# Dilated window attention followed by a multiplicative feed-forward: eight PSUM banks in one set, another turn of w3, another load order

## The chip, the cores and the metric

The kernel runs on one core of a Trainium2 chip. A core has five engines that work side by side, each with its own queue of instructions, done strictly in order: TensorE (PE) multiplies matrices; VectorE (DVE) and ScalarE (ACT) do elementwise work; GpSimd (POOL) here builds masks and issues the loads that convert fp32 to bf16 on the way; SyncE (SP) issues the stores and the DMA transposes. Engines wait for each other through semaphores. Operands lie in SBUF, and PE writes its results to PSUM, which has eight banks; a bank can be written again once its last reader is done. The metric is the device time of one execution in microseconds (us). The median before is 265.82 us (three runs, 264.5 to 266.85).

## The reference

```python
# q, k, v: (8 batches, 8 heads, 576 tokens, 64), fp32
scores = matmul(q, k^T) / 8
rel = pos[:, None] - pos[None, :]
mask_plain = (rel >= 0) & (rel < 32)                       # heads 0 to 3
mask_dil   = (rel >= 0) & (rel < 128) & (rel % 4 == 0)     # heads 4 to 7
attn = softmax(where(mask, scores, -1e9))
x = (attn @ v) as (4608 tokens, 512)
h = (x @ w1) * (x @ w2)              # w1, w2: 512 x 1024
out = (h @ w3) @ w_out               # w3: 1024 x 1024, w_out: 1024 x 512
```

A token sees 32 keys: the last 32 tokens (plain heads), or every fourth of the last 128 (dilated heads). Sorted by its remainder modulo 4, a dilated head is a plain one.

## The kernel before

**The tiling.** The 8 heads are two groups of four, `u` = 0 (plain) and `u` = 1 (dilated), and each group of a batch has six blocks of 96 queries against 128 keys. A `Step(b, u, hf)` is three blocks of four heads, so a batch has four steps, numbered 0 to 3 (0 and 1 are the plain halves, 2 and 3 the dilated ones). In the dilated group the tokens lie sorted by remainder, in runs of 144 (`RUN`), so step 2 holds the first two runs and step 3 the last two.

**One step.** q and k arrive as rows and are turned by DVE (`turn`, L289: whole, or in two parts for some shapes) to have the head dimension on the partitions. `scores` (L342) writes 24 small matmuls into a tile of four PSUM banks; for the first two batches (`BIASED`) four matmuls with an identity first add a mask as a bias. `exps` (L373) is one ACT exponential over 1152 columns; for the other batches `masks` (L377) multiplies the result by a 0/1 mask on DVE. `values` (L383) is 12 matmuls in two halves with a column of ones beside v, so that the sum of the weights comes along; `recip` and `norm` (L405, L419) divide, on DVE, in two halves. Then x is turned back: for the first two batches (`TURNED`) by PE and an ACT copy (`back`, `keep`, L441 and L450), for the others by a DMA transpose that SP issues (`back_dma`, L453). v comes for batches 0 and 1 as rows that DVE and PE turn (`v_back`, `v_keep`, L313 and L323), and for the others directly by strided loads (`load_v_plain`, `load_v_dil`), with a copy of the overlap (`halo_v`).

**The feed-forward.** The tokens are 16 units of 288, unit `k` being half `k % 2` of batch `k // 2`. Unit `k` needs steps 0, 1 and 2 + `k % 2` of its batch. For each unit and each of eight slices `f` of the hidden width, `up` (L470) makes four matmuls with w1, and four with w2; `copy_a` (ACT) and `gate` (DVE) multiply the two. `w3` and `w_out` are fused once: each of eight row slabs of w3 (256 KB in bf16) is turned (`w3_back` on PE, `w3_keep` on ACT) and multiplied by `w_out` (`w3_mul`, L539, then `w3_done`, L551). `down` (L496) multiplies a tile of 128 gated tokens with the fused weight; `copy_y` and `store` follow. Every `down` waits for all eight `w3_done`.

**The order.** It is written out by a planner (`Plan`, L50). Each piece of work is a task with an engine, an assumed duration, its dependences, an assumed latency to users on other engines and a priority; the planner walks through its own clock, gives each free engine the ready task of lowest priority number, and the instructions are then issued in that order. A task with `slot` also needs a free PSUM place. Before, there are four such places of one bank each (`ps_f`), and a separate tile of four banks for the scores (`ps_s`), so that a score step waits until the exponential before it has read the four banks. `RANK` sets the priorities of attention tasks, and `LEAD` how many batches attention runs ahead: the score step `i` of batch `b` comes after pair number `int(16 * (b - LEAD) + 4 * i)` of `up` (16 pairs a batch).

**The loads.** POOL issues, in this order: q, k, v of batch 0, group 0; identity and mask; q, k, v of group 1; w1 and w2, in two halves of 512 columns; w_out in two halves; the eight slabs of w3; q, k, v of batch 1; then the later batches as buffers come free. An issue waits until the load eight places earlier has landed.

Of the kernel before, what the change touches and what calls it, by code (L numbers as in the profile page):

```python
# [10 lines left out]
P = 128  # L11
# [8 lines left out]
S = 576  # L20
# [10 lines left out]
TURNED = 2  # L31
ORDER = (2, 3, 0, 1)
RANK = dict(E=2, VK=1.5, K=1.5, N=0.5, T=3, VT=0.1, S=0.3, V=0.3, X=0.3)
WARM = 16
VKE = (0, 0, 1, 1)
LEAD = 2.25
# [13 lines left out]
class Plan:  # L50
# [5 lines left out]
    def __init__(self, places):  # L56
        self.tasks, self.places, self.now = [], places, None

    def add(self, name, eng, dur, deps, fn, prio, slot=False, lat=150, after=()):
        t = Task(name, eng, dur, deps, fn, prio, slot, lat, after)  # L60
        self.tasks.append(t)
        return t

    def run(self):
# [15 lines left out]
        n, held = len(self.tasks), [None] * self.places  # L80
        now, order, dma = 0.0, [], 0.0

        def freed(t):
            ends = [u.end for u in takers[id(t)]] if t else []
            return None if None in ends else max(ends, default=-200.0) + 100

        while len(order) < n:
            progress = True
            while progress:
                progress = False  # L90
                for e in engines:
                    if free[e] > now:
                        continue
                    at = [freed(t) for t in held]
                    open_ = [(x, i) for i, x in enumerate(at) if x is not None and x <= now]
                    best = None
                    for r, t in waiting[e]:
                        if r > now or (t.slot and not open_):
                            continue
                        if best is None or t.prio < best[1].prio:  # L100
                            best = (r, t)
                    if best is None:
                        continue
                    t = best[1]
                    waiting[e].remove(best)
                    t.start = now
                    if e == "DMA":
                        free[e] = now + t.dur[0]
                        dma = max(dma, now + t.dur[0]) + t.dur[1]
                        t.end = dma + 1900  # L110
                    else:
                        t.end = free[e] = now + t.dur
                    if t.slot:
                        t.place = min(open_)[1]
                        held[t.place] = t
# [18 lines left out]
def kernel(  # L134
# [23 lines left out]
    plan = Plan(places=4)  # L158
# [4 lines left out]
    w3_pool = ctx.enter_context(tc.tile_pool(name="w3", bufs=8))  # L163
    ps_s = ctx.enter_context(tc.tile_pool(name="pss", bufs=1, space=bass.MemoryType.PSUM))
    ps_f = ctx.enter_context(tc.tile_pool(name="psf", bufs=1, space=bass.MemoryType.PSUM))
# [11 lines left out]
    mask = const.tile([P, 7, QB], BF16, name="mask")  # L177
    vps = [const.tile([P, H, 6, PITCH], BF16, name=f"vp{i}") for i in range(2)]
    bias = const.tile([P, 7, QB], BF16, name="bias")
    ets = [const.tile([P, 4 * VC + 32], BF16, name=f"et{i}") for i in range(4)]  # L180
# [5 lines left out]
    def bank(shape, dtype, name):  # L186
        return ps_f.tile(shape, dtype, tag=f"f{plan.now.place or 0}", name=name)
# [5 lines left out]
    def load_rows(nm, src, b, us):  # L193
        if (nm, b) not in qk:
            qk[(nm, b)] = qk_pool.tile([P, 2, 18 * D], BF16, tag=nm, name=nm)
        flat = src[b].rearrange("(u h) s d -> u (h s d)", u=2)
        flat = flat.rearrange("u (p x) -> p u x", p=P)
        nc.gpsimd.dma_start(out=qk[(nm, b)][:, us, :], in_=flat[:, us, :])

# [11 lines left out]
    def load_v_dil(b, m):  # L211
        vp = vps[b % 2]
        r, mu = 2 * (m // 3), m % 3
        runs = {
            0: [(0, 96, r, 0)],
            1: [(0, 48, r, 96), (48, 48, r + 1, 0)],
            2: [(0, 96, r + 1, 48)],
# [11 lines left out]
    def load_w(dst, src, c):  # L229
        f = slice(512 * c, 512 * (c + 1))  # L230
        nc.gpsimd.dma_start(
            out=dst[:, :, f], in_=src[:, f].rearrange("(a p) f -> p a f", p=P)
        )
# [32 lines left out]
    def blocks():  # L266
# [4 lines left out]
        by_res = base.rearrange("p (t r) -> p r t", r=4)  # L271
        nc.scalar.copy(
            out=bias[:, 0:4, :].rearrange("p i (r t) -> p i r t", r=4),
            in_=by_res.unsqueeze(1).to_broadcast([P, 4, 4, 24]),
        )
# [6 lines left out]
    def masks_of_bias():  # L282
        nc.vector.tensor_scalar(
            out=mask, in0=bias, scalar1=0.0, scalar2=None, op0=AL.is_ge
        )
# [3 lines left out]
    def turn(b, u, nm, part):  # L289

# [3 lines left out]
        if part is None:  # L294
# [3 lines left out]
        n, first, odd = ((5, 0, 2 * RUN + 4), (4, 2 * RUN, 5 - 2 * RUN))[part]  # L298
        o = bass.AP(
            tensor=d.tensor,  # L300
            offset=d.offset + pad + first,
            ap=[d.ap[0], [1, n], [RUN, 2], [9, 16], [odd, 2]],
# [3 lines left out]
            offset=src.offset + part * 64,  # L306
            ap=[src.ap[0], [128, n], [32, 2], [1, 32]],
# [5 lines left out]
    def v_back(b, u, half):  # L313
        x = bank([P, 3, 2, P], BF16, "vx")
# [8 lines left out]
    def v_keep(b, u, half, eng):  # L323
        dst = vps[b % 2][:, 4 * u : 4 * u + 4, 3 * half : 3 * half + 3, 0:D]
        for mm in range(3):
            o = dst[:, :, mm, :].rearrange("p h (j c) -> p h j c", c=2)
            i = spread[(b, u, half)][:, mm, :, :].rearrange("p c (h j) -> p h j c", h=4)
            if eng == "ACT":
                nc.scalar.copy(out=o, in_=i)
            else:  # L330
                nc.vector.tensor_copy(out=o, in_=i)  # L331

    class Step:
        def __init__(self, b, u, hf):
            self.b, self.u, self.hf = b, u, hf
            self.et = ets[2 * u + hf]

        def kind(self):
            first = 4 if self.u else self.hf
            return slice(first, first + 3)  # L340

        def scores(self, biased=False):  # L342
            b, u, hf = self.b, self.u, self.hf
            qt, kt = qts[b % 2], kts[b % 2]
            self.sp = ps_s.tile([P, 4, 512], F32, tag="s", name="sp")
            if biased:
                for g in range(4):
                    nc.tensor.matmul(  # L348
                        out=self.sp[:, g, 0:VC],
                        lhsT=ident,  # L350
                        rhs=bias[:, self.kind(), :],
# [3 lines left out]
            for mm in range(3):  # L355
                m = 3 * hf + mm
                for c in range(2):
                    for g in range(4):
# [4 lines left out]
                        else:  # L363
                            qq = qt[prt, u, QB * m : QB * m + QB, c]
                        nc.tensor.matmul(  # L365
                            out=self.sp[:, g, QB * mm : QB * mm + QB],
# [3 lines left out]
                            stop=(c == 1 and (mm == 2 or not biased)),  # L370
                        )

        def exps(self):  # L373
            ev = self.et[:, 0 : 4 * VC].rearrange("p (g x) -> p g x", g=4)
            nc.scalar.activation(out=ev, in_=self.sp[:, :, 0:VC], func=ACT.Exp, scale=scale)  # L375

        def masks(self):  # L377
            ev = self.et[:, 0 : 4 * VC].rearrange("p (g x) -> p g x", g=4)
            mk = mask[:, self.kind(), :].rearrange("p m x -> p (m x)")
            mk = mk.unsqueeze(1).to_broadcast([P, 4, VC])  # L380
            nc.vector.tensor_tensor(out=ev, in0=ev, in1=mk, op=AL.mult)  # L381

        def values(self, pg=None):  # L383

            vp = vps[self.b % 2]
            if pg is None:
                o = self.sp[:, :, VC : VC + 3 * (D + 1)].rearrange("p g (m e) -> p g m e", m=3)
                self.o = [o[:, 0:2, :, :], o[:, 2:4, :, :]]
                gs = range(4)
            else:  # L390
                if pg == 0:
                    self.o = [None, None]
                self.o[pg] = bank([P, 2, 3, D + 1], F32, "vo")
                gs = (2 * pg, 2 * pg + 1)
            for g in gs:
                for mm in range(3):
                    c0 = (3 * g + mm) * QB
                    nc.tensor.matmul(  # L398
                        out=self.o[g // 2][:, g % 2, mm, :],
                        lhsT=self.et[:, c0 : c0 + P],  # L400
                        rhs=vp[:, 4 * self.u + g, 3 * self.hf + mm, 0 : D + 1],
# [4 lines left out]
        def recip(self, pg=None):  # L406
            if pg in (None, 0):
                self.rcp = wk_pool.tile([P, 4, 3], F32, tag="rcp", bufs=4, name="rcp")
                self.xo = wk_pool.tile([P, 12 * D], BF16, tag="xo", bufs=4, name="xo")
            if pg is None:  # L410
                o = self.sp[0:QB, :, VC : VC + 3 * (D + 1)].rearrange(
                    "p g (m e) -> p g m e", m=3
                )
                nc.vector.reciprocal(out=self.rcp[0:QB, :, :], in_=o[:, :, :, D])
            else:
                nc.vector.reciprocal(  # L416
                    out=self.rcp[0:QB, 2 * pg : 2 * pg + 2, :], in_=self.o[pg][0:QB, :, :, D]
                )

        def norm(self, pg):  # L420
            gs = slice(2 * pg, 2 * pg + 2)
            if self.u == 0:
                dst = self.xo[0:QB, :].rearrange("p (m g d) -> p g m d", m=3, g=4)[:, gs, :, :]
            else:
                dst = self.xo[0:QB, :].rearrange("p (q m g d) -> p q g m d", q=2, m=3, g=2)
                dst = dst[:, pg, :, :, :]
            nc.vector.tensor_tensor(  # L427
                out=dst,
                in0=self.o[pg][0:QB, :, :, 0:D],
                in1=self.rcp[0:QB, gs, :].unsqueeze(3).to_broadcast([QB, 2, 3, D]),  # L430
# [10 lines left out]
        def back(self):  # L441
            self.x = bank([P, 6 * QB], BF16, "x")
# [7 lines left out]
        def keep(self):  # L450
            nc.scalar.copy(out=self.cols(), in_=self.x)  # L451
# [345 lines left out]
```

## Time and profile before

| | us |
|---|---|
| median of three runs | 265.82 |
| the profiled execution | 265.6 |
| its span | 263.8 |
| PE, DVE, ACT, POOL busy | 250.6, 172.6, 122.3, 62.7 |
| `up` matmuls (L473), first and last start | 23.1, 254.3 |
| `w3_back` on PE (L530), eight runs of 8 | 35.1 to 50.2 |
| DMA loads from 35 to 54 us | 205 GB/s |
| DMA from 200 to 254 us | 57 GB/s |

The profile is one execution. "PE" and "PEld" are the matmuls and the weight loads of TensorE. A group row gives the line, engine, operation, output from input with shapes and number, then busy time and the mean of one in ns, then idle time before it and what ended it. Matmuls overlap in their pipeline, so the pace of a run of matmuls is read from the chain of waits, which gives pieces as "start, length, what", and not from the mean of one. The busy rows of the page cut the span into 40 slices of 6.6 us, each a digit in tenths. The DMA rows give the time from issue to landing.

### The profile page before, as it was taken

The page shows a single profiled execution, that of the slowest core. Times are in us where ns is not written, and L with a number is a line of the kernel's source. Part 1 is how long each engine was busy: PE and PEld are TensorE (multiplying, and loading weights), DVE is VectorE, ACT ScalarE, POOL GpSimd, SP SyncE. Part 2 cuts the span into 40 slices and gives each one's busy share as a digit, 9 for nine tenths or more (in the row PEclk, how much of TensorE's full clock was granted, in tenths as well). Part 3 has the DMA queues.
Part 4 walks back from the last instruction along what each step waited for, and adds up shares of the span by engine and source line. Part 5 has one row for each costly group of instructions (what it writes and reads, how often), then busy time and mean ns, then how long its engine had stood idle before and what let it go on. Part 6 is the DMA issues. An engine that isn't in the chain of part 4 may idle for free.

```text
span 263.8 us, 6783 instructions
## 1 busy us (share of the span) xinstructions
PE 250.6 (95%) x2736; PEld 168.2 (64%) x2736; DVE 172.6 (65%) x383; ACT 122.3 (46%) x228; POOL 62.7 (24%) x98
## 2 busy tenths in 40 slices
PE   7477999999999999999999999999999999999993
PEld 3365775566667667657667676667676766777661
DVE  3986433899999899989898997455565322233320
ACT  3545354456738444653545444455452342433331
POOL 8612362241726436226313300000000000000000
PEclk9979999999999999999999999999999999999999
DMA  6999999999999959999999934225232112112113
GB/s 99 190 206 207 209 210 212 203 85 216 161 142 148 157 81 210 171 146 202 161 169 149 155 72 65 89 79 62 66 65 62 42 47 73 47 44 73 40 40 119
DMA packets 58030, 32.81 MB, mean 124 GB/s; under 512 B 44688, under 2 KB 47760, under 8 KB 58000
## 3 DMA queue, kind: packets, MB, share of 16 engines
q0 software_dynamic: 37776, 19.40, 58.1%
q1 hardware_dynamic: 20224, 12.98, 25.2%
q8 instruction: 21, 0.34, 0.5%
q14 instruction: 9, 0.07, 0.2%
HBM read 38.80 MB, written 9.44 MB: 183 GB/s over the span
## 4 chain that ended last, share of the span: by engine, by line
PE 77%; DMA 8%; DVE 7%; issue 3%; POOL 2%; ACT 1%; POOLq 0%; DVEq 0%; ACTq 0%
PE ab L473 43%; PE y L500 20%; DMA vp<-in_v_dram 5%; PE wf L542 5%; PE vo L398 3%; PE sp L365 3%; DMA qn<-in_q_dram 2%; DVE xo L427 1%; DVE qt L309 1%; PE x L530 1%; DVE vp L331 1%; DVE kt L309 1%; POOL vp L220 1%; PE sp L348 1%; PE x L444 1%
## 5 line engine op out<-in xcount | busy, mean ns | idle before, releaser
L473 PE MATMUL ab<-XT,w_sb 128*128 128x288 bf16 x1024 | 138.0, 286 | 1.2 <-ACT XT L451 0.7
L473 PEld LDWEIGHTS <-w_sb 128*128 128x128 bf16 x1024 | 96.5, 98 | 31.2 <-issue 1.7
L489 DVE TENSOR_TENSOR gt<-ab,asb 128x288 bf16<-128x288 f32 x128 | 57.9, 454 | 58.0 <-PE ab L473 56.2
L484 ACT CAST asb<-ab 128x288 bf16<-128x288 f32 x128 | 51.1, 400 | 50.6 <-PE ab L473 49.0
L500 PE MATMUL y<-wf_sb,gt 128*128 128x512 bf16 x288 | 67.7, 379 | 0.6 <-DVE vp L331 0.5
L511 ACT COPY osb<-y 128x512 f32<-128x512 f32 x36 | 21.1, 586 | 59.3 <-PE y L500 55.3
L500 PEld LDWEIGHTS <-gt 128*128 128x128 bf16 x288 | 27.8, 98 | 28.5 <-DVE vp L331 0.7
L375 ACT ACTIVATE et<-sp 128x1152 bf16<-128x1152 f32 x32 | 36.4, 1137 | 14.1 <-PE sp L365 14.1
L220 POOL DMA_DIRECT2D vp<-in_v_dram x48 | 31.4, 659 | 45.8 <-PE vo L398 17.7
L427 DVE TENSOR_TENSOR xo<-vo,rcp 96x384 bf16<-96x384 f32 x64 | 35.1, 551 | 1.9
L309 DVE STREAM_TRANSPOSE qt<-qn 128x320 uint32<-128x320 uint32 (+1 forms) x32 | 21.5, 681 | 3.3 <-DMA qn<-in_q_dram 3.0
L398 PEld LDWEIGHTS <-et 128*128 128x128 bf16 x384 | 15.9, 99 | 4.3 <-ACT et L375 0.9
L381 DVE TENSOR_TENSOR et<-et,mask 128x1152 bf16<-128x1152 bf16 x24 | 18.0, 752 | 1.0 <-ACT et L375 0.4
L398 PE MATMUL vo<-vp,et 128*128 128x65 bf16 x384 | 17.6, 195 | 0.9 <-ACT et L375 0.8
L416 DVE RECIPROCAL rcp<-vo 96x6 f32<-96x6 f32 x64 | 11.5, 182 | 8.3 <-PE vo L398 7.9
L542 PE MATMUL wf<-wo_sb,w3T 128*128 128x512 bf16 x64 | 15.0, 379 | 0.0
L365 PEld LDWEIGHTS <-kt 32*128 32x128 bf16 x768 | 9.6, 94 | 7.7 <-issue 7.2
L365 PE MATMUL sp<-qt,kt 32*128 32x96 bf16 x768 | 14.3, 204 | 0.0
L537 ACT COPY w3T<-x 128x1024 bf16<-128x1024 bf16 x8 | 8.1, 1012 | 7.7 <-PE x L530 7.6
L309 DVE STREAM_TRANSPOSE kt<-kn 128x320 uint32<-128x320 uint32 (+1 forms) x16 | 10.9, 681 | 0.1
L552 DVE CAST wf_sb<-wf 128x512 bf16<-128x512 f32 x8 | 5.5, 692 | 7.4 <-PE wf L542 7.4
L296 DVE STREAM_TRANSPOSE kt<-kn 128x576 uint32<-128x576 uint32 x8 | 9.9, 1240 | 0.0
(46 smaller groups left out, 104.2 us busy)
## 6 DMA issues: line engine op xcount, KB each, us to landing
qn<-in_q_dram POOLq DMA_DIRECT2D x7, 576.0 KB, 9.6
kn<-in_k_dram POOLq DMA_DIRECT2D x7, 576.0 KB, 7.9
w_sb<-in_moe_w_dram POOLq DMA_DIRECT2D x4, 512.0 KB, 13.6
w3n<-in_moe_w_dram POOLq DMA_DIRECT2D x8, 256.0 KB, 14.3
out_dram<-osb SPq DMA_DIRECT2D x8, 256.0 KB, 3.4
out_dram<-osb SPq DMA_DIRECT2D x8, 224.0 KB, 2.4
vp<-in_v_dram POOLq DMA_DIRECT2D x6, 288.0 KB, 12.9
out_dram<-osb SPq DMA_DIRECT2D x8, 192.0 KB, 2.5
```

Source lines behind the costliest of these rows:

```text
L220: nc.gpsimd.dma_start(out=vp[32 + p0 : 32 + p0 + n, 4:8, m, 0:D], in_=v_rows(b, 4, 4 * t0 + res, [[4 * D, n], [S * D, 4], [1, D]]),)
L309: nc.vector.transpose(out=o, in_=i)
L365: nc.tensor.matmul(out=self.sp[:, g, QB * mm : QB * mm + QB], lhsT=kt[prt, u, QB * m : QB * m + P, c], rhs=qq, start=(c == 0 and not biase ...
L375: nc.scalar.activation(out=ev, in_=self.sp[:, :, 0:VC], func=ACT.Exp, scale=scale)
L398: nc.tensor.matmul(out=self.o[g // 2][:, g % 2, mm, :], lhsT=self.et[:, c0 : c0 + P], rhs=vp[:, 4 * self.u + g, 3 * self.hf + mm, 0 : D + ...
L427: nc.vector.tensor_tensor(out=dst, in0=self.o[pg][0:QB, :, :, 0:D], in1=self.rcp[0:QB, gs, :].unsqueeze(3).to_broadcast([QB, 2, 3, D]), op ...
L473: nc.tensor.matmul(out=ps, lhsT=w_sb[:, c, f * P : (f + 1) * P], rhs=unit_cols(k, c), start=(j == 0), stop=(j == DCH - 1),)
L484: nc.scalar.copy(out=a_sb, in_=held[("a", k, f)])
L489: nc.vector.tensor_tensor(out=gt[:, f, c0 : c0 + UNIT].rearrange("p (r m t) -> p m r t", r=2, m=BLK), in0=held[("b", k, f)].rearrange("p ( ...
L500: nc.tensor.matmul(out=y, lhsT=gt[:, f, c0 : c0 + P], rhs=wf_sb[:, f, :], start=(f == 0), stop=(f == KFF - 1),)
L511: nc.scalar.copy(out=o_sb, in_=held[("y", i)])
L542: nc.tensor.matmul(out=ps, lhsT=w3T[ft][:, g, :], rhs=wo_sb[:, g, :], start=(g == 0), stop=(g == KFF - 1),)
```

## The change

- **PSUM.** The two pools become one tile of eight banks. A task takes one, two or four places; a score step takes four neighbouring banks (0 to 3 or 4 to 7), `values` two banks at once. `Plan.run` gets a function `place` that picks them.
- **Blocks in groups.** For batches 2 to 7 scores, exponential and mask work on groups of five blocks (`Group`, `GRP = 5`), which can cross steps and batches; a `Step` then gathers its three blocks. `masks` is two halves on DVE. `values` is 12 matmuls in one go, `recip` one instruction of 12 columns, `norm` one instruction for plain steps and two for dilated ones.
- **First q and k.** For batch 0, group 0, SP loads q and k as fp32 into the space of the gated tokens (`load_whole`), and ACT rounds them to bf16 (`round_rows`). POOL's first load is then v.
- **Even tokens first.** The remainders are laid in the order 0, 2, 1, 3 (`RES`), and group 1 of batch 0 is turned in four parts per tensor, even remainders ahead of odd ones, so that step 2 can go before step 3's part is turned. The first two units alternate: slices 0 to 3 of unit 0, of unit 1, then 4 to 7 of both.
- **w3.** Each slab is turned by a DMA transpose that SP issues (`w3_turn`), into one of three buffers. Five of the eight `w3_done` go from DVE to ACT.
- **Loads.** w1 and w2 come as 256, 256 and 512 columns; one slab of w3 comes after the first of these; batch 1 comes before w_out and the other slabs; the last slab waits for a buffer, as there are seven.
- **Smaller.** `v_keep` is one copy of four dimensions in place of three; some `keep` and `v_keep` copies move to DVE; the 0/1 masks are made by POOL in five instructions in place of one on DVE; six buffers in place of four between `copy_a` and `gate`; `LEAD` is 1.3 in place of 2.25, with other priorities.

```diff
-RANK = dict(E=2, VK=1.5, K=1.5, N=0.5, T=3, VT=0.1, S=0.3, V=0.3, X=0.3)
+RES = (0, 2, 1, 3)
+RANK = dict(E=2, VK=2, K=1.5, N=0.3, T=0.5, VT=0.4, S=0.1, V=0.2, X=0.4)
-VKE = (0, 0, 1, 1)
-LEAD = 2.25
+FIRST_LOADS = ("w0", "30", "w1", "w2", "q1", "k1", "v1", "31", "o0", "o1", "32", "33", "34", "35", "36", "37")
+ON_DVE = ("K0.1", "K0.2", "K0.3", "K1.2", "VK1.0.0", "VK1.1.0", "VK1.1.1", "W3D2", "W3D3", "W3D4")
+GRP = 5
+WHOLE = ("qn", "kn")
+LEAD = 1.3
...
+            if t.slot == 4:
+                halves = [h for h in (0, 4) if all(ok[h : h + 4])]
+                if halves:
+                    return halves[0]
...
-    w3_pool = ctx.enter_context(tc.tile_pool(name="w3", bufs=8))
-    ps_s = ctx.enter_context(tc.tile_pool(name="pss", bufs=1, space=bass.MemoryType.PSUM))
-    ps_f = ctx.enter_context(tc.tile_pool(name="psf", bufs=1, space=bass.MemoryType.PSUM))
+    w3_pool = ctx.enter_context(tc.tile_pool(name="w3", bufs=7))
+    ps_pool = ctx.enter_context(tc.tile_pool(name="ps", bufs=1, space=bass.MemoryType.PSUM))
+    ps = ps_pool.tile([P, 8, 512], F32, name="ps")
...
+    def load_whole(nm, src, u):
+        at = {"qn": 0, "kn": 18 * D, "vn": 36 * D}[nm]
+        flat = src[0].rearrange("(u h) s d -> u (h s d)", u=2)
+        flat = flat.rearrange("u (p x) -> p u x", p=P)
+        nc.sync.dma_start(out=stage[:, at : at + 18 * D], in_=flat[:, u, :])
+
+    def round_rows(nm, u):
...
+        nc.scalar.copy(out=qk[(nm, 0)][:, u, :], in_=stage[:, at : at + 18 * D])
...
-        n, first, odd = ((5, 0, 2 * RUN + 4), (4, 2 * RUN, 5 - 2 * RUN))[part]
+        n, first, odd = ((5, 0, RUN + 4), (4, RUN, 5 - RUN))[part % 2]
+        low = max(0, part // 2 - 1)
+        both = 2 if part < 2 else 1
...
-    def w3_back(ft):
-        x = bank([P, KFF, P], BF16, "x3")
-        for g in range(KFF):
-            nc.tensor.transpose(
-                out=x[:, g, :], in_=w3n[ft][:, g * P : (g + 1) * P], identity=ident
-            )
-        held[("x3", ft)] = x
-
-    def w3_keep(ft):
-        w3T[ft] = wk_pool.tile([P, KFF, P], BF16, tag="w3T", bufs=2, name="w3T")
-        nc.scalar.copy(out=w3T[ft], in_=held[("x3", ft)])
+    def w3_turn(ft):
+        w3T[ft] = wk_pool.tile([P, KFF, P], BF16, tag="w3T", bufs=3, name="w3T")
+        nc.sync.dma_start_transpose(out=w3T[ft], in_=w3n[ft])
...
+        x = add(f"XW{ft}", "SP", 100, [lw3[ft]], lambda f=ft: w3_turn(f), -1, lat=3600,
+                after=[w3m[-3] if len(w3m) > 2 else None])
+        if ft + 7 in lw3:
+            lw3[ft + 7].after.append(x)
+            lw3[ft + 7].deps.append(x)
+        z = add(f"W3M{ft}", "PE", 1728, [x, lwo[0], lwo[1]], lambda f=ft: w3_mul(f), 7, slot=1)
...
+    half = KFF // 2
+    begin = [(k, f + h) for h in (0, half) for k in range(2) for f in range(half)]
```

## The prediction

> **What bounds the kernel now.** I read the page first, then the chain of waits in order of time, short windows over the head, the groups by shape, and the DMA answers.
>
> ```profile
> span 263.8 us, 6783 instructions
> PE 250.6 (95%) x2736; PEld 168.2 (64%) x2736; DVE 172.6 (65%) x383; ACT 122.3 (46%) x228; POOL 62.7 (24%) x98
> PE   7477999999999999999999999999999999999993
> q1 hardware_dynamic: 20224, 12.98, 25.2%
> ```
>
> By the busy digits TensorE (PE) is the bound after the first four slices of 6.6 us. The chain gives the instants and the price of one piece of the stream:
>
> ```profile
> 23.12 0.65 PE ab L473 x4
> ...
> 41.08 0.45 PE x L530 x8
> 41.52 1.73 PE wf L542 x8
> ...
> 96.51 0.38 PE sp L365 x24
> 96.89 1.58 PE ab L473 x12
> ...
> 99.92 0.36 PE vo L398 x12
> ...
> 254.54 5.19 PE y L500 x24
> 259.80 0.59 ACT osb L511
> ```
>
> The first FFN matmul is at 23.12, the last ends at 259.73, 4.1 us before the end. In between the stream costs: 256 `up` at 0.49 (four matmuls; 24 take 2.94 in the chain) = 125.4; 36 `down` and 8 `w3_mul` at 1.73 = 76.1; 8 `w3_back` at 0.45 = 3.6; 24 unbiased score steps at 0.375 = 9.0; batch 1's four biased ones at 0.95 = 3.8, its v turns 1.4, back-transposes 1.4; 28 value steps at 0.365 = 10.2. Sum 230.9 of 236.6: 5.7 us is lost in small holes. So 263.8 = 23.1 + 230.9 + 5.7 + 4.1. The execution took 265.6 us with 1.8 outside the span, by the median of 265.82. 1% of that (2.7 us) is what a measurement can tell from no change.
>
> The head is a chain over VectorE (DVE), with a clock that falls (windows of 1 us: busy us of PE, PEld, DVE, ACT, POOL, then granted clock, DMA share, GB/s):
>
> ```profile
> 13.00:14.00 1.00, 0.00 (x0) 0.00 (x0) 0.94 (x4) 0.77 (x1) 0.39 (x1) 1.00 1.25 206
> 14.00:15.00 1.00, 0.49 (x5) 0.37 (x6) 0.96 (x3) 0.00 (x0) 0.16 (x1) 0.87 1.24 205
> 15.00:16.00 1.00, 1.00 (x17) 0.91 (x16) 0.96 (x3) 0.64 (x1) 0.00 (x0) 0.50 1.24 213
> ```
>
> **Part by part.** (1) `w3` turned by DMA: eight `w3_back` leave PE, −3.6, and eight 1.01 us copies leave ACT, which is no bound (46%), so nothing.
>
> (2) The head. DVE decides when unit 0 can start, by these rows:
>
> ```profile
> L309 DVE STREAM_TRANSPOSE qt<-qn 128x320 uint32<-128x320 uint32 x16 | 11.7, 734 | 3.0 <-DMA qn<-in_q_dram 3.0
> L309 DVE STREAM_TRANSPOSE qt<-qn 128x256 uint32<-128x256 uint32 x16 | 10.0, 628 | 0.3
> L296 DVE STREAM_TRANSPOSE kt<-kn 128x576 uint32<-128x576 uint32 x8 | 9.9, 1240 | 0.0
> L427 DVE TENSOR_TENSOR xo<-vo,rcp 96x384 bf16<-96x384 f32 x64 | 35.1, 551 | 1.9
> ```
>
> Before, DVE starts on q at 5.54. Now q comes by SP: the queue is free at about 0.7, landing takes between the 2.4 us of a store and the 4.3 us of the first q load (I take 4.2, the nearest row), then an ACT rounding of 1152 elements: 1.14 like the exponential of that size, and not before the bias copies end at 5.1. So DVE starts at about 6.3, 0.8 later. In the built order follow: q 1.4, k 1.24, v 1.24; then five turns of half a head group (q even, k even, q odd, v even, k odd). From the three sizes a transposition is about 0.17 us plus 1.85 ns an element, so a pair of half-size parts is 0.86, five 4.3: 14.5. Reciprocal and one 768-element norm 1.14 (15.6), v odd 0.86 (16.5), another 1.14 (17.6), a reciprocal and two 384-element norms 1.3 (18.9), two PSUM copies `keep`, 0.46 (a gate) to 0.64 (on ACT) each, 1.1: 20.0. PE and ACT results for these come earlier by the same durations, because the second score step no longer waits for the first exponential (two sets of four banks). With 0.5 for hand-overs, unit 0 starts at 20.5: −2.6 (bounds −3.6 and −1). Its weights are now 256 columns wide and early enough: before, 512 KB took 2.55 us each from 17.7, so 2×256 KB are there by about 17.
>
> (3) The clock. In the rows above PE idles 1.42 and 0.47 us, and the granted clock is 0.50 from 15 to 18. In the new head PE has about 1.3 us of work in the 3.4 us before unit 0, so a fall there would put the first 3.4 us of `up` at half speed: 0 to +1.7; I take +0.8. The Trainium skill (TensorE: Matmul & The Clock Gate, HAM oscillation) asks for a gap above about 3.4 us before the clock halves. By it this term would be 0; the row, which fell after 1.42, decides.
>
> (4) Load order. In the window 35 to 54 us loads run at 205 GB/s, so an early load is paid by a later one. Before, `w12` landed by 24.8, `w_out` 29.8, `w3` 40, batch 1 by 48.5. With the same pace: batch 1 by 34, one `w3` slab 35.3, `w_out` 40.4, five slabs 41.7 to 46.7. Unit 0 and 1 need 32 `up` = 15.7 us, PE is free at about 37 and batch 1's attention must then run nearly bare: four score steps 3.8, v turns 1.4, values 1.5, two `w3_mul` 3.5, back-transposes 0.8, in a chain score, exponential (1.14), v copy (1.0), value that takes until 49.5. That is 11.0 of 12.4: +1.4 (0.5 to 2.8). Against it, the holes of 54 to 92 us, where batches 1 and 2 were squeezed in before (by the same piece prices some 2.0), go: −2.0.
>
> (5) Slabs turned. The nearest row:
>
> ```profile
> XT<-xo SPq DMA_TRANSPOSE x24, 4.8
> ```
>
> ```profile
> DMA to landing us min/median/max: 2.4/4.8/11.2
> ```
>
> That is 144 KB; a slab is 256 KB, times 1.78: 4.3, 8.5 or 20 us. Three buffers mean that slab 3 goes when `w3_mul` 0 ends (46.3), slab 4 at 48.3, slab 5 after `w3_mul` 2 (54.6). In the built order six `up` and a back-transpose stand between `w3_mul` 1 and 2, then 2, 3 and 4 follow each other, then six `up` and a score step come before 5; so PE reaches `w3_mul` 2 to 6 at about 52.9, 54.6, 56.4, 62 and 65, with the other `up` of batch 1 queued behind them. At 8.5 us slabs 3 to 5 are 0.3, 0.2 and 0.5 late: +1.0 (0 to +12, see the rival). The skill (DMA: Bandwidth & Descriptors, Latency and other measured facts) gives 261 GB/s for such a transposition. That would be about 1.0 us a slab and a term of 0.
>
> (6) What they take from the loads. Stores in 210 to 250 use 0.17 of the 16 engines for 53 GB/s, 3.2 us a MB; 9.44 MB are 30 of the 66.5 us of the hardware queue. The rest is 36 us for 24 transpositions, 1.5 each, 2.7 a slab; nothing is the other bound. Five slabs lie before k of batch 2, which would land at 52.3 (53.6 less one slab), so 52.3 to 65.8. The score step of batch 2 (at 59) needs it at 57.6 with DVE's turn; half of the cost leaves it at 59. The wait for q stands on DVE ahead of `w3_done` and of gates. +0.8 (0 to +8).
>
> (7) Five-block groups, one 12-column reciprocal, masks on POOL, gates six deep: DVE loses about 0.8 of 22 us a batch, and scores come later (LEAD 1.3 instead of 2.25), so DVE's 53.6 of 58 us between 92 and 150 thins out. Of the remaining 3.7 us of holes I take −1.0 (−2 to +1). POOL's masks stand before batch 2's v loads; POOL waits there for earlier loads anyway (9.1 us in four waits), without that up to 4.5 us by the 0.28 of 96 elements. Half-turning costs DVE's fixed 0.17 three times, inside (2). ACT's new `w3_done` (0.59) hides under its 54% idle.
>
> SP's queue holds the eight slabs ahead of the first `back_dma` and the first store, both later than `w3_mul` 7 would let them be anyway; nothing else stands behind them.
>
> Sum: −3.6 −2.6 +0.8 +1.4 −2.0 +1.0 +0.8 −1.0 = −5.2. Span 258.6, time 260.4.
>
> **Rivals.** A: covers hold. Clock 0, bare stretch +0.5, slabs and loads 0, holes −2: −9.7, 255.9 us. For it: every stall in (3), (5), (6) rests on one bound. Against: holes exist before too. Chance 0.23.
> B, slower: slabs land late. The 11.2 and the 20 us show how transpositions fare beside loads. At 14 us slabs 2 to 6 hold PE 2.8, 3.0, 0.3, 3.3 and 2.4 us, 11.8 against the 1.0: 271.2. It decides from a landing of about 12 us. Against: the median. Chance 0.16.
> C: given back. Clock +1.7, bare +2.8, slabs +3, loads +1.5, holes 0, with the fixed −3.6, −2.6, −2.0: +0.8, 266.4 us. Also what is seen if the early start only moves PE's wait to batch 1's loads. Chance 0.16.
>
> **Numbers.** The forecast (258 to 263.1) has 0.45. Faster is it and A, 0.68; same C, 0.16; slower B, 0.16. The range goes from a little under A, 254.5, to where B decides, 268.5.
>
> **What would show it.** First `up` at 20 to 21 us and its clock; no `w3` transposes on PE; PE holes between 37 and 50 of 1 to 3 us and their releaser; landing of the slabs, 5 to 9 us; whether PE or DVE waits for batch 2's q and k near 55 to 62; a last `down` that ends near 254.5. A first `up` after 22, or slabs above 12 us, make it wrong.

## The result, and the profile after

| | before | after |
|---|---|---|
| median | 265.76 | 277.31 (274.29 to 278.63, four runs) |
| the profiled execution | 265.6 | 274.29 |
| its span | 263.8 | 272.5 |
| first `up` starts | 23.12 | 18.83 |
| last `down` ends | 259.73 | 268.06 |

The changed kernel is slower: the ratio is 1.0398, with an interval of 1.0298 to 1.0498. The profiled execution is the shortest of its four, so the trace shows some 3 us less of the loss than the median. Its page first:

```profile
span 272.5 us, 6621 instructions
...
PE 247.4 (91%) x2672; PEld 165.2 (61%) x2672; DVE 164.7 (60%) x340; ACT 115.7 (42%) x208; POOL 66.2 (24%) x103
...
PE   8679896099599997999999999999999999999993
...
PEclk9999999569979999999999999999999999999998
...
PE 70%; DMA 24%; POOL 2%; ACT 1%; issue 1%; DVE 0%; SPq 0%; DVEq 0%; POOLq 0%; ACTq 0%
```

The head (the first four digits of PE) is a little denser than before, and from slice 17 on nothing has changed. The digits 6, 0 and 5 of slices 7, 8 and 11 (41 to 54 and 68 to 75 us) are new, with a granted clock of 0.5 and 0.6 after the first of them. The last line is the chain of waits by engine: a quarter of it goes through DMA. Not all of that is idle time of PE: while slab 1 loads, which is on the chain until 36.67 us, PE has other work. The timeline of PE (start, length, what, and in brackets the idle time before it and what ended it) shows where:

```profile
18.83 1.63 PE L526 MATMUL ps<-XT,w_sb 128*128 128x288 bf16 x12 [0.18 <-DVE XT L504]
...
53.87 3.60 PE L587 MATMUL ps<-wo_sb,w3T 128*128 128x512 bf16 x8 [8.60 <-DMA w3T<-w3n]
...
75.34 3.14 PE L587 MATMUL ps<-wo_sb,w3T 128*128 128x512 bf16 x8 [3.19 <-DMA w3T<-w3n]
...
262.72 5.34 PE L553 MATMUL ps<-wf_sb,gt 128*128 128x512 bf16 x24
```

`w3_mul` (now L587) of slab 1 waits 8.60 us for its transposed slab, that of slab 5 3.19, and both run at about half speed: eight matmuls take 3.60 and 3.14 us in place of 1.73. The chain, in order of time, says what those slabs waited for:

```profile
16.14 20.51 DMA w3n<-in_moe_w_dram
36.67 17.15 DMA w3T<-w3n
53.87 3.60 PE ps L587 x8
...
64.09 11.20 DMA w3T<-w3n
75.34 3.14 PE ps L587 x8
```

Slab 1 is loaded by 36.67, and its transposition goes out that instant; it lands 17.15 us later. No other slab was in flight beside it at first: slab 0 (issued at 15.9, 15.4 us) had landed, and slab 2 goes out at 43.5. The DMA view gives both kinds of transposition (number, median us from issue to landing), and the slabs' own answer their extremes:

```profile
XT<-xo SPq DMA_TRANSPOSE x24, 2.9
...
w3T<-w3n SPq DMA_TRANSPOSE x8, 11.4
```

```profile
DMA to landing us min/median/max: 8.6/11.4/17.1
```

Meanwhile the DMA goes on (windows; the last three columns are granted clock, DMA share and GB/s of all queues):

```profile
45.00:50.00 5.00, 0.27 (x7) 0.12 (x3) 1.62 (x3) 1.13 (x2) 3.79 (x6) 0.85 0.99 176
50.00:55.00 5.00, 1.13 (x3) 0.44 (x4) 0.00 (x0) 0.00 (x0) 1.37 (x3) 0.50 1.15 199
55.00:60.00 5.00, 5.00 (x39) 3.23 (x38) 1.31 (x4) 1.42 (x3) 0.59 (x1) 0.62 1.66 140
```

PE, DVE and ACT stand still together, while the DMA moves 176 and 199 GB/s. Its queues in the first two of these windows (packets, that is pieces of transfers, then MB and share of the 16 engines; "software" is POOL's queue of loads, "hardware" is SP's):

```profile
q0 software_dynamic: 400, 0.78, 83.0%
q1 hardware_dynamic: 398, 0.10, 15.6%
```

```profile
q0 software_dynamic: 569, 0.86, 93.8%
q1 hardware_dynamic: 576, 0.14, 21.6%
```

The two queues move the same number of packets, but a packet of the loads has some 1500 to 2000 bytes and one of a transposition some 250. So most of the bytes that move are the loads'. They pay little: from 35 to 55 us their queue moves 3.54 MB, where it moves 3.89 in e1 (below), which has no transposed slabs, and q and k of batch 2 land after 16.7 us, in e1 after 13.6 and 13.9.

The account of the span against before: the head −4.3; between the first `up` and the end of the last `down` +12.6 (249.2 for 236.6); the tail +0.4. The middle has 3.6 less to do, so its losses grew by 16.2. The page's waits put 12.2 of them to the slabs, and the two slow `w3_mul` cost 1.87 and 1.41 more than 1.73: 15.4 in all.

### The profile page after: what moved, and what is told of

It is laid out like the page before. It is cut to its first block, busy times and chain, and to the rows that moved or that the text cites. A ratio compares the mean times of both kernels' runs of the same rounds, so it can differ in the third digit from the quotient of the medians.

```text
span 272.5 us, 6621 instructions
## 1 busy us (share of the span) xinstructions
PE 247.4 (91%) x2672; PEld 165.2 (61%) x2672; DVE 164.7 (60%) x340; ACT 115.7 (42%) x208; POOL 66.2 (24%) x103
## 4 chain that ended last, share of the span: by engine, by line
PE 70%; DMA 24%; POOL 2%; ACT 1%; issue 1%; DVE 0%; SPq 0%; DVEq 0%; POOLq 0%; ACTq 0%
PE ps L526 39%; PE ps L553 20%; DMA w3n<-in_moe_w_dram 11%; DMA w3T<-w3n 10%; PE ps L587 4%; PE ps L454 3%; DMA out_dram<-osb 3%; PE ps L418 3%; ACT et L429 1%; ACT osb L564 1%; POOL w_sb L279 1%; PE ps L494 0%; POOL vn L232 0%; DVE vp L276 0%; POOL qn L232 0%
## 5 line engine op out<-in xcount | busy, mean ns | idle before, releaser
L526 PE MATMUL ps<-XT,w_sb 128*128 128x288 bf16 x1024 | 135.9, 286 | 1.2 <-DVE gt L542 0.8
L542 DVE TENSOR_TENSOR gt<-ps,asb 128x288 bf16<-128x288 f32 x128 | 58.0, 454 | 59.2 <-PE ps L526 52.8
L537 ACT CAST asb<-ps 128x288 bf16<-128x288 f32 x128 | 50.8, 398 | 65.7 <-PE ps L526 60.8
L553 PE MATMUL ps<-wf_sb,gt 128*128 128x512 bf16 x288 | 67.4, 379 | 0.0
L564 ACT COPY osb<-ps 128x512 f32<-128x512 f32 x36 | 21.1, 585 | 57.2 <-PE ps L553 49.6
L429 ACT ACTIVATE et<-ps 128x1920 bf16<-128x1920 f32 (+2 forms) x23 | 34.4, 1508 | 5.7 <-PE ps L418 4.7
L477 DVE TENSOR_TENSOR xo<-ps,rcp 96x384 bf16<-96x384 f32 (+1 forms) x48 | 31.6, 676 | 0.6
L587 PE MATMUL ps<-wo_sb,w3T 128*128 128x512 bf16 x64 | 17.9, 434 | 12.2 <-DMA w3T<-w3n 12.2
L437 DVE TENSOR_TENSOR et<-et,mask 128x960 bf16<-128x960 bf16 (+1 forms) x30 | 18.5, 633 | 12.7 <-ACT et L429 12.4
L367 DVE STREAM_TRANSPOSE qt<-qn 128x320 uint32<-128x320 uint32 (+3 forms) x34 | 22.5, 665 | 2.8 <-DMA qn<-in_q_dram 1.6
L587 PEld LDWEIGHTS <-w3T 128*128 128x128 bf16 x64 | 6.4, 106 | 20.8 <-DMA w3T<-w3n 13.1
L454 PE MATMUL ps<-vp,et 128*128 128x65 bf16 x384 | 15.7, 195 | 1.8 <-DVE vp L276 1.4
```

What stands on the lines that cost most here:

```text
L367: nc.vector.transpose(out=o, in_=i)
L429: nc.scalar.activation(out=ev, in_=self.sp[:, :, 0:x], func=ACT.Exp, scale=scale)
L454: nc.tensor.matmul(out=self.o[:, g, mm, :], lhsT=grp.et[:, c0 : c0 + P], rhs=vps[self.b % 2][:, 4 * self.u + g, 3 * self.hf + mm, 0 : D + ...
L477: nc.vector.tensor_tensor(out=dst, in0=self.o[0:QB, hs, :, 0:D], in1=self.rcp[0:QB, hs, :].unsqueeze(3).to_broadcast([QB, n, 3, D]), op=AL ...
L526: nc.tensor.matmul(out=o, lhsT=w_sb[:, c, f * P : (f + 1) * P], rhs=unit_cols(k, c), start=(j == 0), stop=(j == DCH - 1),)
L537: nc.scalar.copy(out=a_sb, in_=held[("a", k, f)])
```

## The experiments

Each kernel was run beside runs of the kernel before, whose median was within 265.4 and 265.8. The order of work is planned anew in each, so that single effects do not add up exactly. The theory put to the test is that the transposed slabs land late because loads are in flight, and that PE, which works strictly in order, stands behind them. Its rivals: the slowness lies elsewhere in the change; a slab takes that long by its size alone; the planner's assumed latency of 3.6 us puts `w3_mul` too early; the half clock is the cost.

**e1: w3 turned on PE again, all else as changed**

```diff
-        x = add(f"XW{ft}", "SP", 100, [lw3[ft]], lambda f=ft: w3_turn(f), -1, lat=3600, ...
+        x = add(f"W3T{ft}", "PE", 510, [lw3[ft], idt], lambda f=ft: w3_back(f), 6, slot=1, ...
+        y = add(f"W3C{ft}", "ACT", 1012, [x], lambda f=ft: w3_keep(f), -1, lat=100, ...
```

> The changed kernel with one part undone: w3 is turned by eight runs of PE transposes and eight ACT copies again, everything else stays, the order is planned anew. Theory A (DMA transposes beside saturated loads land late, 11 to 17 us, and PE stands in order behind them): the holes of 8.6, 3.2 and 0.4 us before w3_mul and some 4 us of half-clock after them go, 3.6 us of PE work comes back: 272.5 - 12.2 - 4 + 3.6 = about 260 span, 261.7 us, no PE idle above 2 us between 40 and 80. Theory B (batch 1 ahead of w_out and w3 makes the slabs themselves late): the holes stay, PE waits for loads of w3 instead, 270 us or more.

Measured: 257.51 us (257.5 to 257.87), ratio 0.9716 (0.9676 to 0.9756). It is the best version of all, faster than both kernels, and 4 us under the 261.7 expected, so more than the waits and the slow matmuls came back. The same 20 us in both kernels, first after, then e1 (columns: busy PE, PEld, DVE, ACT, POOL; clock, DMA share, GB/s):

```profile
35.00:55.00 20.00, 10.81 (x197) 7.21 (x196) 10.84 (x18) 6.53 (x8) 11.60 (x15) 0.84 1.17 196
```

```profile
35.00:55.00 20.00, 19.25 (x295) 13.04 (x297) 16.18 (x29) 13.10 (x16) 11.90 (x16) 1.00 1.34 198
```

With the DMA at the same 196 and 198 GB/s PE is busy 19.25 us, where it was busy 10.81. In e1's chain a slab costs its transposition and its product, and nothing between:

```profile
52.63 0.45 PE ps L583 x8
53.08 1.73 PE ps L595 x8
54.81 0.45 PE ps L583 x8
```

So the DMA transposes of w3 alone cost 19.8 us net by the medians (277.31 less 257.51), although they save 3.6 us of PE. The rest of the change is worth −8.1.

**e2: the kernel before, with w3 turned by DMA and nothing else**

```diff
-    def w3_back(ft):
...
-    def w3_keep(ft):
...
+    def w3_turn(ft):
+        w3T[ft] = wk_pool.tile([P, KFF, P], BF16, tag="w3T", bufs=3, name="w3T")
+        nc.sync.dma_start_transpose(out=w3T[ft], in_=w3n[ft])
...
+        y = add(f"XW{ft}", "SP", 100, [lw3[ft]], lambda f=ft: w3_turn(f), -1, lat=6900, ...
```

> The kernel before with one part of the change alone: w3 turned by DMA transposes from SP into three buffers, old load order. Theory A: slabs land from 31 us on, while loads run at 205 GB/s until 48, so transpositions take 11 us or more there; three in flight, eight slabs: w3_mul ends at 65 us or later instead of 53.5, slower than before, 270 to 282 us. Theory B: the old order has the slabs early, the transpositions are no matter, 3.6 us of PE work is gone: 261 to 264 us.

Measured: 286.76 us, one run, above the expected 270 to 282. The timeline of PE, then the slabs' landings:

```profile
48.05 0.61 PE L534 MATMUL wf<-wo_sb,w3T 128*128 128x512 bf16 x1 [8.70 <-DMA w3T<-w3n]
...
57.75 3.59 PE L534 MATMUL wf<-wo_sb,w3T 128*128 128x512 bf16 x8 [6.11 <-DMA w3T<-w3n]
```

```profile
DMA to landing us min/median/max: 2.7/8.9/25.5
```

The loss does not need the rest of the change. Here the first two slabs, issued at 31 to 32 us, land after 17 to 25 us; the last four, issued after 61, when the loads had thinned out, after 2.7 to 7.0.

**e3: four more slab transpositions late in the execution**

```diff
+    for i in (24, 27, 30, 32):
+        add(f"quiet{i}", "SP", 100, [Y[i]], extra, 0)   # a slab once more, into a spare buffer
```

Nothing reads their result.

> The changed kernel with four more transpositions of a w3 slab whose results nobody reads, after the 25th, 28th, 31st and 33rd down, when no loads run. Theory A: each lands in 4 to 5.5 us (the 2.4 to 2.9 us of a quiet 144 KB transposition times 1.78). Theory C (a slab costs that much by itself, whatever runs beside): 8.6 us or more, as the shortest of the eight. Time 273 to 279 under both.

Measured: 273.08 us, one run, a little below the four runs of after. SP's timeline has the last two at 244 and 256 us; the slabs' answer for 250 to 272 us has the landing of the last:

```profile
244.44 1.29 SPq L869 DMA_TRANSPOSE w3T<-w3n  x1
256.04 1.35 SPq L869 DMA_TRANSPOSE w3T<-w3n  x1
```

```profile
DMA to landing us min/median/max: 3.1/3.1/3.1
```

The first of the four lands after 4.5 us, the others after 3.1 to 3.4, less than the 4 to 5.5 expected for these three. The eight slabs of the same execution took 7.7 to 16.6 earlier: it isn't the size.

**e6: the loads of batches 2 and 3 held back until slab 6 is turned**

```diff
+    def hold():        # on POOL, ahead of the loads; reads two columns of the turned slab 6
+        nc.gpsimd.tensor_scalar(out=warm[:, 0:2], in0=w3T[6][:, 0, 0:2], ..., op0=AL.is_ge)
```

> The changed kernel with POOL held, by one two-column instruction that reads the seventh turned slab, before the loads of batches 2 and 3; so no load is in flight from about 50 us until that slab has landed. Theory A (the transposition waits its turn among the packets of loads): slabs 1 and 2, turned while w_out and the other slabs still load, land as late as in the changed kernel (12 to 17 us), slabs 3 to 6 in 3 to 5 us. If a transposition is slow early in the kernel for another reason (SP's issue, the buffers): all stay at 9 us or more. The whole kernel is slower than the changed one in any case, as batch 2 comes late: 278 to 290 us.

Measured: 283.65 us, one run. What it is to show are the landings, here from the slabs' own answer for 30 to 45 us and for 62 to 70:

```profile
L582 SPq DMA_TRANSPOSE w3T<-w3n x2: 1948/2792/3637, 35.6 to 43.3; - x2
...
DMA to landing us min/median/max: 8.9/12.3/15.7
...
L582 SPq DMA_TRANSPOSE w3T<-w3n x3: 1231/1232/1232, 61.3 to 64.8; - x3
...
DMA to landing us min/median/max: 3.0/3.1/3.1
```

Two slabs go out while the first loads still run, and take 15.7 and 8.9 us; the next, issued at 47.1 while the last loads end, takes 6.0; once none is in flight, three take 3.0 to 3.1, and the time that SP spends on the issue falls as well (the first figures, in ns: 1948 to 3637, then 1232). Same kernel, same queue, some 20 us apart. The kernel as a whole loses: batch 2 comes late, and the held loads now meet the stores of the first `down`. The chain has one of these, and the timeline of PE the longest wait of this run, which follows from it:

```profile
98.18 14.42 DMA out_dram<-osb
```

```profile
113.34 0.99 PE L418 MATMUL ps<-qt,kt 32*128 32x96 bf16 x40 [11.30 <-ACT osb L564]
```

A store of at most 256 KB takes 14.42 us, beside loads that bring the DMA to 212 GB/s from 98 to 112 us; until it is out, ACT can't empty a bank that a score step needs. Holding the loads shows the cause but is no cure.

**e5: the planner told of a longer latency**

```diff
-    lat=3600
+    lat=8100
```

> The changed kernel with one planner constant changed: the assumed latency of a w3 transposition is 8.1 us in place of 3.6 (11.4 with the addition for busy queues, the measured median), so that PE gets other work ahead of each w3_mul. Theory A, with the loss in the order that PE is held to: landings stay at 9 to 17 us, holes before w3_mul shrink to under 6 us together, 266 to 272 us. If the loss is in the DMA time that the transpositions take from loads: holes move to the score and value steps of batch 2, 274 us or more.

Measured: 273.81 us, one run, which can't be told from after. The timeline of PE:

```profile
54.20 3.59 PE L587 MATMUL ps<-wo_sb,w3T 128*128 128x512 bf16 x8 [6.03 <-DMA w3T<-w3n]
...
79.87 1.90 PE L587 MATMUL ps<-wo_sb,w3T 128*128 128x512 bf16 x7 [1.78 <-DMA w3T<-w3n]
...
82.77 1.90 PE L587 MATMUL ps<-wo_sb,w3T 128*128 128x512 bf16 x8 [0.99 <-DMA w3T<-w3n]
...
105.66 0.78 PE L454 MATMUL ps<-vp,et 128*128 128x65 bf16 x18 [2.24 <-ACT osb L564]
```

The holes before `w3_mul` fall from 12.2 to 8.8 us, as a better place in the order would have it, but the slabs now land after 9.4 to 17.0, and a new wait comes at 105.66: on the chain stands a store that goes out at 95.47 and takes 9.45 us, so that ACT, and PE behind it, get no buffer. The order is a small part; the expected 266 to 272 was missed. Latencies still longer were not tried.

**e10: the clock kept up through the holes**

```diff
+        fill = {1: 38, 5: 14}.get(ft)      # so many matmuls on a zero tile ahead of w3_mul
+            x = add(f"fill{ft}", "PE", 10, [x, lwo[0], lwo[1]], lambda n=fill: keep_warm(n), 6.9, slot=1)
```

> The changed kernel with 38 and 14 matmuls on zeros put into its two long holes, right ahead of the second and the sixth w3_mul (8.2 and 3.0 us at full clock), so that PE does not idle there. If the half clock after the holes is a cost of its own (8 w3_mul took 3.5 us instead of 1.73 after the first hole, 3.1 after the second, and the matmuls beside them longer too): the matmuls after the holes run at full pace and the kernel gains 3 to 4.5 us on the changed one's 277.3 us, 273 to 274.5. If landings set the path all the way: the gain is taken by later waits, 276 to 278.

Measured: 278.15 us (276.08 to 280.42), ratio 1.0423 (1.0332 to 1.0513). The timeline of PE:

```profile
45.40 8.37 PE L614 MATMUL ps<-warm 128*128 128x512 bf16 x38
...
55.23 1.90 PE L587 MATMUL ps<-wo_sb,w3T 128*128 128x512 bf16 x8 [1.46 <-DMA w3T<-w3n]
...
68.52 1.90 PE L587 MATMUL ps<-wo_sb,w3T 128*128 128x512 bf16 x8 [3.52 <-DMA w3T<-w3n]
```

The clock is 1.00 in all the profiled execution, and eight matmuls take 1.9 us where they took 3.60; but slab 1 lands after 18.0 us, PE waits for slabs as before, and the time doesn't fall: it is near the 276 to 278 expected if the landings set the path. What a full clock saves in one `w3_mul` is lost at the next slab.

**The parts that helped.** Five runs on e1, which is free of the slabs' loss, undo one part each. What a part is worth is the difference of the medians; every run of the five is longer than every run of e1, but for `WHOLE`, `LEAD` and `GRP` the interval of the ratio overlaps e1's (0.9676 to 0.9756), so these three values are rough.

*The load order of before:*

```diff
-FIRST_LOADS = ("w0", "30", "w1", "w2", "q1", "k1", "v1", "31", "o0", ...)
+FIRST_LOADS = ("w0", "w1", "w2", "o0", "o1", "30", ..., "36", "q1", "k1", "v1", "37")
```

> The first experiment's kernel (w3 turned on PE) with the old order of loads: w1, w2, w_out, seven slabs of w3, then batch 1, then the last slab. If batch 1 first is worth what fills PE between 35 and 55 (batch 1 lands near 47 instead of 35, but the eight w3_mul can fill the time): same to slower, 257.5 to 261 us. If the order of loads was a second cause of the loss: faster, 254 to 256.5.

Measured: 260.86 us (260.0 to 261.83), ratio 0.984 (0.9798 to 0.9883). The new order is worth 3.4.

*Scores kept to banks 0 to 3, all else to 4 to 7:*

```diff
-                halves = [h for h in (0, 4) if all(ok[h : h + 4])]
+                halves = [h for h in (0,) if all(ok[h : h + 4])]
...
-            at = [i for i in range(8) if ok[i] and (kept is None or i // 4 != kept // 4)]
+            at = [i for i in range(4, 8) if ok[i]]
```

> The first experiment's kernel with the eight banks split as before: score groups only in banks 0 to 3, all else in 4 to 7. If the common set is what shortens the head and batch 1 (second score step before the first exponential): first up 1 to 1.5 us later, batch 1 about 1 us longer, 259 to 262 us. If it is worth nothing: 257 to 258.5.

Measured: 266.9 us (266.87 to 268.87), ratio 1.0073 (1.0032 to 1.0114), far above the 259 to 262 expected. The common set is worth 9.4 us. Of it 1.8 is in the head: the first `up` starts at 20.98 instead of 19.22. Timelines of PE, of e8 and then e1:

```profile
8.86 0.44 PE L416 MATMUL ps<-qt,kt 32*128 32x96 bf16 x24 [0.89 <-DVE kt L350]
...
10.62 0.65 PE L399 MATMUL ps<-bias,ident 128*128 128x288 bf16 x4
```

```profile
9.18 0.44 PE L418 MATMUL ps<-qt,kt 32*128 32x96 bf16 x24 [1.40 <-DVE kt L352]
9.55 0.66 PE L401 MATMUL ps<-bias,ident 128*128 128x288 bf16 x4
```

With a second set of four banks the next score step (its bias comes first) follows at once, 0.37 us after the scores before it have begun; with one set it starts 1.76 us after them, when the exponential has read the banks. The other 7 us are hardly seen among PE's waits. They are in its busy time, as the groups of lines show for the same 1024 `up` and 384 value matmuls (busy us, mean ns, idle before), e8 and then e1:

```profile
L524 PE MATMUL ps<-XT,w_sb 128*128 128x288 bf16 x1024 | 139.4, 286 | 2.5 <-DVE xo L475 0.6 <-DVE gt L540 0.6 <-ACT asb L535 0.5
...
L452 PE MATMUL ps<-vp,et 128*128 128x65 bf16 x384 | 17.0, 193 | 0.4 <-ACT et L427 0.2
```

```profile
L526 PE MATMUL ps<-XT,w_sb 128*128 128x288 bf16 x1024 | 135.2, 286 | 0.2 <-DVE XT L504 0.2
...
L454 PE MATMUL ps<-vp,et 128*128 128x65 bf16 x384 | 15.2, 193 | 0.1
```

The matmuls are as long one by one, but they follow each other less closely: 4.2 and 1.8 us. In e8's chain an `up` at 71.67 starts when a `copy_a` (from 71.22, 0.41 us) ends, and the next at 72.94 when a `gate` (from 72.43, 0.47 us) ends; these two are what frees a bank of `up`. The run lands 1 us above before's time, so without the common set the rest of the change wins nothing.

*q and k of the first group as bf16 by POOL, as before* (`WHOLE = ()`):

> The first experiment's kernel with q and k of batch 0, group 0, loaded by POOL with conversion again. DVE can start 0.8 us earlier on q, but the next four loads are issued two places later: first up at 18.5 to 20.5, 257 to 259.5 us.

Measured: 259.15 us (258.61 to 261.68), ratio 0.9794 (0.9737 to 0.985). Worth 1.6. The first `up` starts at 21.75 in the profiled execution, later than expected; but that execution is the longest of the four (261.68), and its clock was 0.50 from 16 to 18 us, so how much of the 1.6 lies in the head is not shown.

*Attention as far ahead as before* (`LEAD = 2.25`):

> The first experiment's kernel with LEAD 2.25 as before, so attention runs further ahead. The prediction gave the later attention 1 us of gain from a less crowded DVE: then 258 to 260. If pacing is worth nothing: 257 to 258.

Measured: 259.87 us (259.85 to 259.89), ratio 0.9762 (0.9708 to 0.9816). Worth 2.4.

*Groups of three blocks* (`GRP = 3`):

> The first experiment's kernel with score groups of three blocks as before in place of five. ACT then spends about 1.14 x 4 instead of 1.81 x 2.4 us a batch, DVE about the same; neither is the bound: 257 to 259. If the longer groups matter through the four-bank halves they hold (fewer turns of them): 259 or more.

Measured: 260.39 us (260.37 to 260.41), ratio 0.9781 (0.9736 to 0.9827). Worth 2.9. The five single values make 19.7, more than the 8.1 of all together, so they can't be added.

## Why the prediction was wrong

The forecast had the wrong sign. Rival B, slabs that land late, was the mechanism, at 0.16.

**The step that failed is (5), slabs turned.** It took 4.8 us, the median of the 24 transpositions of before, times 1.78: 8.5 us a slab and +1.0. Measured, a slab took 8.6 to 17.1 us, 11.4 in the median, and the term was 15.4 us in the profiled execution: 12.2 of waits and 3.3 of slow `w3_mul`. Two things went wrong there.

The row was the right operation, but its median mixes two surroundings. In the trace of before, six of the 24 go out from 100 to 125 us, with the DMA at 182 GB/s, and seven from 150 to 200, at 72:

```profile
L454 SPq DMA_TRANSPOSE XT<-xo x6: 1237/1508/2005, 101.9 to 122.7; - x6
...
DMA to landing us min/median/max: 7.1/7.7/8.8
```

```profile
L454 SPq DMA_TRANSPOSE XT<-xo x7: 1196/1205/2401, 154.7 to 194.8; - x7
...
DMA to landing us min/median/max: 2.4/2.6/4.3
```

The four from 125 to 150 us, at 158 GB/s, take 5.6 to 11.2, 9.3 in the median. The slabs go out into loads at 205 GB/s, so the rows for them are the busy ten: 7.7 and 9.3 times 1.78 are 13.7 and 16.6 us, which is rival B's 14 and more. The factor 1.78 was too large rather than too small: in the quiet a slab takes 3.0 to 3.4 us (e3, e6; once 4.5), where `XT` takes some 2.5.

And the step counted slabs 2 to 6, and slab 1 not at all. Slab 1's load came when predicted (36.7, against 35.3); PE wanted its product at 45.27. By the forecast's own 8.5 us from there it would have landed at 45.2, with nothing to spare, and each us more would have held PE. At 17.15 it made the largest hole, 8.60. Rival B had the right cause with the wrong places: of its 11.8 us on slabs 2 to 6, slab 5 took 3.19 and another one 0.37. Its price, 271.2, was below the 277.31 for the same reason.

The Trainium skill (DMA: Bandwidth & Descriptors, Latency and other measured facts) gives 261 GB/s for such a transposition. By our estimate from it, which counts the bytes alone, a slab is 1.0 us; the shortest landing that any run here shows is 2.7 (e2), and beside the loads it is up to 25.5 (e2). Neither the page's figure nor the median of the kernel is a price for a transposition beside saturated loads.

**(1)** held: eight `w3_back` at 0.45 are gone from PE; e1, which has them again, shows them in its chain at 0.45.

**(2) the head** was right in its first part: q landed after 4.2 us and DVE began at 6.27, against 6.3. It was short in what follows: −4.3 instead of −2.6, more than its bound of −3.6. DVE's transpositions follow one another faster than their durations tell (pairs of half-size parts start 0.78 apart, where 0.86 was taken). On e1's head, undoing the common set of banks cost 1.8, and undoing the fp32 loads 2.5 (21.75 less 19.22), in an execution whose clock fell.

**(3) the clock**: 0 in place of +0.8; it is granted at 1.00 until 45 us. The rule of the skill, by which the term is 0, was right in this execution. But in e9, which is e1 with the first q and k loaded as before, the clock was 0.50 from 16 to 18 us, so the row of before was no false alarm.

**(4) load order**: the bare stretch cost about 0.6 in 35 to 45 us, where +1.4 was taken. By e7 the order is worth −3.4, where the two halves of the step made −0.6.

**(6)** was 0: no wait of PE is for batch 2's q and k. But the step looked at the smaller effect. It asked what the transpositions take from the loads, and that was little (3.54 MB against e1's 3.89 from 35 to 55 us); what the loads took from the transpositions was not asked.

**(7)** was far too small. In e1 the middle, from 19.22 to 251.66, takes 232.4 us, 1.5 more than the 230.9 of work by the prediction's own prices, where before it took 5.7 more. So what (4) and (7) hold removed 4.2 together, where −1.6 was taken. The common set of banks had no price of its own at all beyond a share of the head, though e8 shows that it is the largest part, 9.4. Without (1), (5) and (6), which go with the transposed slabs, so for e1, the prediction's sum is −3.4, 262.2 us; measured 257.51.

**Why the slabs wait.** That a transposition needs the loads out of its way is shown by e3 and e6. The packet counts show much of the way in which it happens. Three slabs in the quiet of e6, from 61 to 68 us, are 3168 packets, so a slab is 1056. Where loads and slabs move side by side, the two queues move as many packets each: 400 and 398, 569 and 576 in the windows above, 1429 and 1438 from 45 to 57 us in e2. So a slab moves at the pace of the loads' packets, 80 to 115 a us in the first two: by our estimate 9 to 13 us for its 1056. Before that come SP's issue, 1.9 us for slab 1, and a wait: from 36.7 to 40.5 us a single packet of SP's queue moves. What that wait is was not followed.

**What stays open.** After's middle takes 249.2 us and e1's 232.4 with 3.6 more work, so the slabs cost 20.4 there. Of these 12.2 are the waits for slabs and 3.3 the two slow `w3_mul`. Some of the rest is in view: the work right behind the slow `w3_mul` runs at the low clock too (0.50 until 58 us, 0.61 from 58 to 59), and a store on the chain takes 7.33 us at 97.53, after which PE idles 1.9 of the 8 us from 104 to 112. How the last few us divide was not followed.

## What to carry to other kernels

Price a DMA by rows from a stretch as busy as the one in which it will run, not by a median over the execution: ask for the rows window by window, count what else is in flight there, and compare the size of the packets, since the queue with the small ones moves the fewer bytes. Where an engine works in order, check every consumer of a moved transfer, the first one above all, for the slack it has at the forecast's own landing time; a transfer with no slack makes the whole sum hang on that one value. When a change of many parts loses, undo them one at a time: here one part cost 19.8 us, and the change without it beats both kernels.

## What the runs showed of the hardware

A DMA transposition and the loads of another queue share by packets and not by bytes: 398 packets of some 250 bytes went beside 400 of some 2 KB (after, 45 to 50 us), 1438 beside 1429 (e2). Beside loads that keep the DMA at 140 to 210 GB/s a 256 KB slab takes from 7.7 us (e3) to 25.5 (e2) to land, with none in flight 3.0 to 3.1 (e6). Where the loads' packets are small as well, from 55 to 60 us in after (1863 packets for 0.26 MB), the transpositions move the more bytes: 0.44 MB. Stores, which SP issues too, are slow beside loads as well: 7.33 (after), 9.45 (e5) and 14.42 us (e6), where the median of after's stores of 256 KB is 2.6; in e6 the two queues moved 1396 and 1407 packets from 98.2 to 112 us. SP's own time for the issue grows too, from 1.2 us a slab to as much as 6.0 in after and 12.2 in e2, and what is queued behind it waits: in after slab 3 goes out at 49.6, as the issue of slab 2 (43.5, 6.0 us) ends.

The clock fell to 0.50 in the hole of 8.60 us, as the Trainium skill has it (TensorE: Matmul & The Clock Gate, HAM oscillation: a gap above about 3.4 us): PE stops at 45.27, and the granted clock is 1.00 until 48, 0.77 from 48 to 49 and 0.50 from 49. After the hole of 3.19 us, a little shorter than that, it was 0.50 too, from 76 to 79 us. In the head of before it fell after idle times of 1.42 and 0.47 us, which that rule does not give. Nor does it seem to fall there every time: of the ten runs of the kernel before beside e6, the two with a mean clock of 1.00 have spans of 262.5 and 262.6 us, the six with 0.993 or 0.994 have 263.4 to 263.9, and the two with 0.987 have 264.9 and 265.4. Three us at half clock, as in the profiled execution, are 1.5 us or 0.006 of the span, so one such fall or two would make these steps; where the clock fell in those runs was not recorded.
